# A decode block over 32 heads: one VectorE step moved by a chunk, the last head's exps moved behind copies, and another order of the first head's late sums

## The chip, the core and the metric

The kernel runs on one core of a Trainium2 chip. The metric is the device time of one launch in microseconds (us). TensorE is called PE here, VectorE DVE, ScalarE ACT, GpSimd POOL and SyncE SP, as in the profile.

## The reference

One token `x` (640 numbers) passes an attention block with a cache and then a dense block, in bf16:

```
q = layernorm(x) @ wq                    # 32 heads x 192
p = softmax(q . k_cache * 192**-0.5)     # per head, over 32768 positions
h = x + (p @ v_cache for all heads) @ wo
out = h + relu(layernorm(h) @ w1) @ w2   # 640 -> 1536 -> 640
```

Each head has 12.6 MB of keys and as much of values, so almost all that the kernel does is to read 805 MB of cache, and to make two products with each element.

## The kernel before, in words

**Tiling.** A head has 32768 positions. They are worked in eight *chunks* (`c` = 0 to 7); a chunk holds 32 positions of each of the 128 partitions. Within a chunk two engines share the scores. For 20 or 16 of the 32 positions PE transposes the keys (`transposes`, L366, into `tp`), ACT copies the result out to `kT` (`copies`, L601), and PE multiplies it with the query (`scores_pe`, L397, into `sp`). For the other 12 or 16 positions DVE multiplies keys and query and sums the products (`scores_dve`, L671: the product is L688 and the sum L691, into `sc`). ACT then takes the exp of both parts: `exp_pe` (L610, into `pB`) and `exp_dve` (L616, into `pA`). Last, PE adds exps times values into `o_ps` (`values`, L417): 16 matmuls per chunk, which wait for both exps and for the chunk's values. Where a text says "the sum of chunk c", it means this step; its label in the code is `PV`.

**End of a head.** The output of head h is finished within head h+1: PE adds up the denominators (`den_mm`), DVE scales the output (`den_rec`, L694 and `o_scale`, L699), PE turns the row into a column (`o_turn`, L453), DVE copies the column out (`o_turned`, L707: L709, then L713, which waits for PE's turn, then L715), and PE multiplies it with `wo` (`project`, L460). In PE's order `o_turn` stands behind the scores of chunk 1, and `project` behind the transposes of chunk 4.

**The order of the work** is written out by hand, an order of its own for each engine. Head 0 is built by itself, heads 1 to 30 are one loop (`looped`, L820), head 31 (`LAST`) is built by itself, with ten smaller chunks at its end (`pe_end`, L543). Engines wait for one another on semaphores, and each engine works in its own order, so an instruction that waits holds up all that stand behind it. `SUMS` and `SUMS_0` (L500, L501) say for heads 1 to 30 and for head 0 in which step PE makes which sums. The last entry holds the sums that stand at the very end of a head.

**The transfers** are all issued by SP in one order (`dma_program`, L230): for each head keys `kt[0]` (6 MB, chunks 0 to 3), values `vb` (3 MB, chunks 0 and 1), keys `kt[1]` (6 MB, chunks 4 to 7), then values of chunks 2 and 3 into `vb` again and values of chunks 4 to 7 (6 MB) into `va`. In head 0 alone the load of `va` stands ahead of the second load of `vb`. A load may only be issued when its buffer is free. That is why SP waits for sums: the first load of `vb` for head h waits until the sum of chunk 3 of head h-1 is done (L253), the second until the sum of chunk 1 of the same head is done. The keys `kt[1]` of a head stand behind that first load of `vb` in SP's order. The last head loads smaller pieces, four value pieces behind its sum of chunk 1, and `w1` and `w2` behind its sum of chunk 3.

**Last head.** ACT's order there is that of `act_head` (L644): copies of chunk c, then both exps of chunk c-1. DVE goes through the nine chunks in which it has a part, and PE through `pe_end`. After the last sum come the denominators, the projection, a second layernorm and the dense block: small instructions, one behind the other.

Of the kernel before, what the change touches and what calls it, by code (L numbers as in the profile page):

```python
# [80 lines left out]
def kernel(  # L81
# [34 lines left out]
    LAST = H - 1  # L116
# [13 lines left out]
    def chunks(h):  # L130
        return ends if h == LAST else full
# [285 lines left out]
    def values(g, h, c):  # L417

        jc, jp, ld, off = chunks(h)[c][2:]
        jd = jc - jp  # L420
        if h == LAST and ld >= NL - 1:
            g.wait("vc", h, c)
        elif h == LAST and ld == 2:
            g.wait("vh", c - 4)
        elif off == 0:
            g.wait("at", "v", h, ld)
        g.wait("ep", h, c)
        if jd > 0:
            g.wait("ed", h, c)
        if c == 0 and h > 0:  # L430
            g.wait("os", h - 1)
        src = v_tile(h, ld)
        a, b = pA[c % NB], pB[c % NB]
        calls = []
        order = list(range(jd, jc, 2)) + list(range(0, jd, 2))
        for i, j in enumerate(order):
            w = a[:, j:j + 2] if j < jd else b[:, j - jd:j - jd + 2]
            calls.append(mmul(o_ps[0:2, 0:2 * Dh], w, src[:, (off + j) * Dh:(off + j + 2) * Dh],
                              start=(c == 0 and i == 0),
                              stop=(c == len(chunks(h)) - 1 and i == len(order) - 1), skip_group_check=True))  # L440
        pe_group(g, calls, ("PV", h, c), "pe")

    def den_mm(g, h):
        g.wait("ep", h, len(chunks(h)) - 1)
        if h < LAST:
            g.wait("ed", h, NC - 1)
            g.wait("qm", h + 1)
        else:
            g.wait("ed", h, NCM - 2)
            g.wait("oTc", h - 1)  # L450
        pe_group(g, [mmul(mm[:, 0:2 * NCM], ones_mat[:], dsums[:], start=True, stop=True)], ("den", h), "pe_dve")
# [33 lines left out]
    def q_spread(g, h, turn=None):  # L485

        hh = h if turn is None else turn
        calls = [mmul(mm[:, e:Dh:2], qe[:, bass.ds(2 * hh + e, 1)].to_broadcast([HE, P]), wide[0:HE, HE:2 * HE],
                      start=(e == 0), stop=(e == 1), skip_group_check=True) for e in range(2)]

        for b in range(3):
            for i in range(2):
                j = (P - HE) * b + (HE if i == 0 else 0)
                calls.append(mmul(mm[:, Dh + 4 * b + i:Dh + 4 * b + i + 3:2], wide[0:HE, j:j + P],
                                  qe[:, bass.ds(2 * hh, 2)], start=True, stop=True))
        pe_group(g, calls, ("qs", h), "pe_act")
# [1 line left out]


    SUMS = ((), (), (0,), (1,), (), (), (2, 3), (4,), (5, 6, 7))  # L500
    SUMS_0 = ((), (), (0,), (1,), (), (), (4,), (5,), (6, 7, 2, 3))  # L501

    def pe_head(g, h, turn=None):
        for c in range(NC + 1):
            if c < NC and c != 4:
                transposes(g, h, c)
            if c == 0 and h > 0:
                den_mm(g, h - 1)
            for d in (SUMS if h > 0 else SUMS_0)[c]:
                if c < NC:  # L510
# [9 lines left out]
            if c == 6:  # L520
                q_spread(g, h + 1, turn)
        for d in (SUMS if h > 0 else SUMS_0)[NC]:
            values(g, h, d)
# [77 lines left out]
    def copies(g, h, c):  # L601
        ld, off, jc, jp = chunks(h)[c][:4]
        t0 = sum(len(tiles(q[3])) for q in chunks(h)[:c])
        for k, (b0, nb) in enumerate(tiles(jp)):
            g.wait("T", h, c, k)
            src = tp[(t0 + k) % TP]
            g.do(lambda: act.copy(out=kT[c % 2][:, b0:b0 + nb, :], in_=src[:, 0:nb, :].bitcast(bf16)),  # L607
                 "act_pe", ("cp", h, c, k))

    def exp_pe(g, h, c):  # L610
        jp = chunks(h)[c][3]
        g.wait("S", h, c)
        g.do(lambda: act.activation(out=pB[c % NB][:, 0:jp], in_=sp[:, 0:jp], func=F.Exp, scale=SCALE,  # L613
                                    accum_out=dsums[:, 2 * c + 1:2 * c + 2]), "act_pe", ("ep", h, c))

    def exp_dve(g, h, c):  # L616
        ld, off, jc, jp = chunks(h)[c][:4]
        jd = jc - jp
        if jd == 0:
            return  # L620
        g.wait("sc", h, c)
        g.do(lambda: act.activation(out=pA[c % NB][:, 0:jd], in_=sc[c % NC][:, 0:jd], func=F.Exp, scale=SCALE,  # L622
                                    accum_out=dsums[:, 2 * c:2 * c + 1]), "act_pe", ("ed", h, c))

    def q_wide(g, h):
        g.wait("qs", h)
        if h > 0:
            g.wait("sc", h - 1, NC - 1)
        g.do(lambda: act.copy(out=qb[:], in_=mm[:, 0:Dh]), "act_dve", ("qb", h))
        g.do(lambda: act.copy(out=qm[:], in_=mm[:, Dh:Dh + 12]), "act_pe", ("qm", h))  # L630
# [12 lines left out]

    def act_head(g, h):  # L644
        q_wide(g, h)
        n = len(chunks(h))
        for c in range(n):
            if c == 4 and h < LAST:
                exp_pe(g, h, 3)
                exp_dve(g, h, 3)  # L650
                copies(g, h, 4)
                continue
            copies(g, h, c)
            if c > 0:
                exp_pe(g, h, c - 1)
                exp_dve(g, h, c - 1)
        exp_pe(g, h, n - 1)
        exp_dve(g, h, n - 1)

    def act_end(g):  # L660
        act_head(g, LAST)
        act_norm(g, "ln2")
        g.wait("h1")
        g.wait("rs", "ln2")
        g.do(lambda: act.activation(out=h1T[:], in_=o_ps[:, 0:FT], func=F.Relu, scale=ln_t["ln2"]["rs"][:]),
             "act_pe", ("h1T",))
# [4 lines left out]
    def scores_dve(g, h, c):  # L671
        ld, off, jc, jp = chunks(h)[c][:4]
        jd = jc - jp
        if jd == 0:
            return
        if h == LAST and ld >= NL - 1:
            g.wait("k", h, ld)
        else:
            g.wait("atd", "k", h, ld)
        if c == 0:  # L680
            g.wait("qb", h)
        if h == LAST and c >= NC:
            g.wait("PV", h, c - NC)
        src = k_tile(h, ld)
        n = -(-jd // JDM)
        for i in range(n):
            j0, j1 = jd * i // n, jd * (i + 1) // n
            g.chain(lambda: dve.tensor_tensor(  # L688
                out=pr[:, 0:j1 - j0, :], in0=src[:, (off + j0) * Dh:(off + j1) * Dh].rearrange("p (j d) -> p j d", d=Dh),
                in1=qb[:].unsqueeze(1).to_broadcast([P, j1 - j0, Dh]), op=A.mult), "dve")  # L690
            g.chain(lambda: dve.reduce_sum(out=sc[c % NC][:, j0:j1], in_=pr[:, 0:j1 - j0, :], axis=X), "dve")  # L691
        g.tell("dve_act", ("sc", h, c))

    def den_rec(g, h):  # L694
        g.wait("den", h)
        g.chain(lambda: dve.reduce_sum(out=rec[:, 0:1], in_=mm[:, 0:2 * NCM], axis=X), "dve")  # L696
        g.chain(lambda: dve.reciprocal(out=rec[:, 1:2], in_=rec[:, 0:1]), "dve", ("rec", h))  # L697

    def o_scale(g, h):  # L699
        if h == LAST:  # L700
            g.wait("PV", h, NCM - 1)
        g.wait("rec", h)
        g.do(lambda: dve.tensor_scalar_mul(out=o_pair[:, :, 1, :],  # L703
                                           in0=o_ps[0:2, 0:2 * Dh].rearrange("q (i d) -> q i d", i=2),
                                           scalar1=rec[0:2, 1:2]), "dve_pe", ("os", h))

    def o_turned(g, h):  # L707

        g.chain(lambda: dve.tensor_scalar(out=odd[:], in0=odd[:], scalar1=-1.0, scalar2=1.0, op0=A.mult, op1=A.add),  # L709
                "dve", ("odd", h))  # L710
        g.wait("oT", h)
        g.wait("odd", h)
        g.do(lambda: dve.tensor_scalar_mul(out=oT[:], in0=mm[:, 0:3], scalar1=odd[:]), "dve_pe", ("oTc", h))  # L713
        if h < LAST:
            g.chain(lambda: dve.tensor_copy(out=o_pair[:, :, 0, :], in_=o_pair[:, :, 1, :]), "dve")  # L715
# [27 lines left out]
    def dve_head(g, h):  # L743
        for c in range(len(chunks(h))):
            scores_dve(g, h, c)
            if c % 4 == 3 and h < LAST:
                g.tell("dve_sp", ("scs", h, c))
            if c == 0 and h > 0:
                den_rec(g, h - 1)
                o_scale(g, h - 1)  # L750
            if c == 1 and h > 0:
                o_turned(g, h - 1)

    def dve_end(g):
# [48 lines left out]
    for e in parts:  # L803
        far = {s: 0 for s in TAKEN[e]}
        ends_at[e] = []
        for h in range(LAST):
            for label in logs[e][h]:
                s, n = at[label]
# [86 lines left out]
```

The softmax here doesn't subtract the row's maximum and nothing guards it: scores larger than these inputs give would overflow.

## Time and profile before

| what | us |
|---|---|
| median of 9 runs | 1928.43 |
| lowest and highest run | 1926.48, 1930.83 |
| the profiled execution | 1927.57 |
| span of its instructions | 1925.8 |
| PE, PEld, DVE, ACT busy | 1554.4, 1093.4, 1560.0, 939.5 |

The span runs from the first to the last instruction that the profile has; the profiled execution's own time is 1.8 us longer. PEld is PE's weight loading, which runs beside its matmuls. In rows of the timeline the columns are: start, duration, engine, line, operation, tiles written and read, count, and in brackets the engine's idle time just before and what ended it. Rows of a table by windows give for each stretch its length, the busy time of PE, PEld, DVE, ACT and POOL (with instruction counts), the granted PE clock, the share of time that the sixteen DMA engines were busy, and GB/s.

### The profile page before, as it was taken

The page shows a single profiled execution, that of the slowest core. Times are in us where ns is not written, and L with a number is a line of the kernel's source. Part 1 is how long each engine was busy: PE and PEld are TensorE (multiplying, and loading weights), DVE is VectorE, ACT ScalarE, POOL GpSimd, SP SyncE. Part 2 cuts the span into 40 slices and gives each one's busy share as a digit, 9 for nine tenths or more (in the row PEclk, how much of TensorE's full clock was granted, in tenths as well). Part 3 has the DMA queues.
Part 4 walks back from the last instruction along what each step waited for, and adds up shares of the span by engine and source line. Part 5 has one row for each costly group of instructions (what it writes and reads, how often), then busy time and mean ns, then how long its engine had stood idle before and what let it go on. Part 6 is the DMA issues. An engine that isn't in the chain of part 4 may idle for free.

```text
span 1925.8 us, 36134 instructions
## 1 busy us (share of the span) xinstructions
PE 1554.4 (81%) x15908; PEld 1093.4 (57%) x15908; DVE 1560.0 (81%) x732; ACT 939.5 (49%) x2000; POOL 1.0 (0%) x6
## 2 busy tenths in 40 slices
PE   7878887887888787878788878878777788878797
PEld 7555565665555565555554556555555556555554
DVE  2797787987878978789887879878788787897886
ACT  2454454554544554545544535545445445455453
POOL 0000000000000000000000000000000000000000
PEclk9888988788988879888889888889888898888988
DMA  9999999999999999999999999999999999999997
GB/s 410 419 423 436 426 437 430 436 434 434 431 432 432 437 431 432 438 428 437 436 430 432 438 429 436 436 431 434 434 435 431 435 429 437 429 437 434 434 427 293
DMA packets 29634, 825.29 MB, mean 429 GB/s; under 512 B 3115, under 2 KB 4652, under 8 KB 8108
## 3 DMA queue, kind: packets, MB, share of 16 engines
q1 hardware_dynamic: 29610, 824.98, 99.3%
q8 instruction: 15, 0.25, 0.0%
q14 instruction: 7, 0.06, 0.0%
q10 hardware_dynamic: 2, 0.00, 0.0%
HBM read 824.97 MB, written 0.00 MB: 428 GB/s over the span
## 4 chain that ended last, share of the span: by engine, by line
DVE 41%; DMA 38%; PE 15%; ACT 5%; issue 1%; DVEq 0%; POOLq 0%; SPq 0%
DMA kt<-in_A_k_cache_dram 34%; DVE sc L691 19%; DVE pr L688 19%; PE o_ps L364 7%; PE tp L383 6%; ACT kT L607 4%; DMA va<-in_A_v_cache_dram 2%; DMA vb<-in_A_v_cache_dram 1%; PE sp L364 1%; DVE o_pair L703 1%; ACT pA L622 0%; DVE oT L713 0%; DMA kt<-in_A_wq_dram 0%; DVE rec L696 0%; DVE rec L697 0%
## 5 line engine op out<-in xcount | busy, mean ns | idle before, releaser
L688 DVE TENSOR_TENSOR pr<-kt,qb 128x2304 f32<-128x2304 bf16 (+2 forms) x257 | 755.9, 2941 | 316.7 <-POOLq L325 288.5
L607 ACT COPY kT<-tp 128x1024 bf16<-128x1024 bf16 (+1 forms) x899 | 814.2, 1015 | 270.4 <-PE tp L383 270.3
L383 PE MATMUL tp<-ident_f,kt 128*128 128x128 f32 x3459 | 598.0, 334 | 249.2 <-POOLq L346 173.7
L691 DVE TENSOR_REDUCE sc<-pr 128x12 f32<-128x2304 f32 (+2 forms) x257 | 755.3, 2939 | 8.9
L383 PEld LDWEIGHTS tp<-ident_f,kt 128*128 128x128 f32 x3459 | 492.8, 173 | 304.2 <-POOLq L346 188.1
L364 PE MATMUL o_ps<-va,pB 128*2 128x384 bf16 x1152 | 221.6, 340 | 61.7 <-POOLq L346 61.5
L364 PEld LDWEIGHTS sp<-qm,kT 128*128 128x128 bf16 x6918 | 197.8, 98 | 81.8 <-issue 43.3
L364 PE MATMUL o_ps<-vb,pB 128*2 128x384 bf16 x1154 | 217.0, 335 | 23.3 <-ACT pA L622 20.3
L364 PE MATMUL sp<-qm,kT 128*128 128x2 bf16 x6918 | 214.6, 164 | 25.0 <-ACT pB L613 24.0
L622 ACT ACTIVATE pA<-sc 128x12 bf16<-128x12 f32 (+2 forms) x257 | 57.9, 225 | 354.2 <-DVEq L65 354.2
L613 ACT ACTIVATE pB<-sp 128x20 bf16<-128x20 f32 (+2 forms) x258 | 51.8, 201 | 311.4 <-PE sp L364 311.3
L364 PEld LDWEIGHTS o_ps<-va,pB 128*2 128x2 bf16 x1152 | 94.1, 86 | 157.9 <-POOLq L346 69.3
L364 PE MATMUL o_ps<-va,pA 128*2 128x384 bf16 x896 | 172.6, 334 | 0.0
L364 PE MATMUL o_ps<-vb,pA 128*2 128x384 bf16 x894 | 166.6, 326 | 0.0
L364 PEld LDWEIGHTS o_ps<-vb,pB 128*2 128x2 bf16 x1154 | 91.0, 85 | 125.6 <-ACT pA L622 26.2
L364 PEld LDWEIGHTS o_ps<-va,pA 128*2 128x2 bf16 x896 | 77.4, 86 | 76.2 <-issue 9.8
L364 PEld LDWEIGHTS o_ps<-vb,pA 128*2 128x2 bf16 x894 | 75.2, 84 | 70.6 <-issue 0.6
L613 ACT ACTIVATION_READ_ACCUMULATOR pB<-sp 128x1 f32 x258 | 54.7, 212 | 0.0
L622 ACT ACTIVATION_READ_ACCUMULATOR pA<-sc 128x1 f32 x257 | 52.7, 205 | 0.0
L364 PE MATMUL o_ps<-xn_ln,kt 128*96 128x1 bf16 (+1 forms) x316 | 22.4, 208 | 2.8 <-DMA kt<-in_A_wq_dram 2.8
L364 PEld LDWEIGHTS o_ps<-xn_ln,kt 128*96 128x96 bf16 (+1 forms) x316 | 22.2, 176 | 2.9 <-issue 2.8
L703 DVE TENSOR_SCALAR o_pair<-o_ps,rec 2x384 bf16<-2x384 f32 x32 | 19.3, 605 | 2.7 <-PE o_ps L364 1.7
(69 smaller groups left out, 188.6 us busy)
## 6 DMA issues: line engine op xcount, KB each, us to landing
kt<-in_A_k_cache_dram SPq DMA_DIRECT2D x62, 6144.0 KB, 25.8
vb<-in_A_v_cache_dram SPq DMA_DIRECT2D x63, 3072.0 KB, 24.8
va<-in_A_v_cache_dram SPq DMA_DIRECT2D x31, 6144.0 KB, 26.8
kt<-in_A_k_cache_dram SPq DMA_DIRECT2D x3, 3072.0 KB, 21.0
wo_s<-in_A_wo_dram SPq DMA_DIRECT2D x16, 480.0 KB, 19.0
kt<-in_A_wq_dram SPq DMA_DIRECT2D x4, 1536.0 KB, 11.0
va<-in_A_v_cache_dram SPq DMA_DIRECT2D x1, 3072.0 KB, 25.3
va<-in_A_v_cache_dram SPq DMA_DIRECT2D x2, 1536.0 KB, 36.0
```

The costliest lines, as they stand in the source:

```text
L364: return lambda: pe.matmul(o, lhsT=w, rhs=r, **kw)
L383: calls.append(lambda b=b, o=o: pe.transpose(out=dst[:, b, :], in_=src[:, o:o + 2 * P].bitcast(f32), identity=ident_f[:]))
L607: g.do(lambda: act.copy(out=kT[c % 2][:, b0:b0 + nb, :], in_=src[:, 0:nb, :].bitcast(bf16)), "act_pe", ("cp", h, c, k))
L613: g.do(lambda: act.activation(out=pB[c % NB][:, 0:jp], in_=sp[:, 0:jp], func=F.Exp, scale=SCALE, accum_out=dsums[:, 2 * c + 1:2 * c + 2]), ...
L622: g.do(lambda: act.activation(out=pA[c % NB][:, 0:jd], in_=sc[c % NC][:, 0:jd], func=F.Exp, scale=SCALE, accum_out=dsums[:, 2 * c:2 * c + ...
L688: g.chain(lambda: dve.tensor_tensor(out=pr[:, 0:j1 - j0, :], in0=src[:, (off + j0) * Dh:(off + j1) * Dh].rearrange("p (j d) -> p j d", d=D ...
L691: g.chain(lambda: dve.reduce_sum(out=sc[c % NC][:, j0:j1], in_=pr[:, 0:j1 - j0, :], axis=X), "dve")
L703: g.do(lambda: dve.tensor_scalar_mul(out=o_pair[:, :, 1, :], in0=o_ps[0:2, 0:2 * Dh].rearrange("q (i d) -> q i d", i=2), scalar1=rec[0:2, ...
```

## The change

Three edits, all in the order of the work; no instruction is added or taken away.

1. In head 0 the four sums at its very end go in the order 2, 3, 6, 7 and not 6, 7, 2, 3.
2. In the last head ACT takes the exp of DVE's part of a chunk one step later: after the copies of the chunk after next, and just ahead of the exp of PE's part of the next chunk. In heads 0 to 30 ACT's order stays.
3. In heads 1 to 31 DVE runs `o_turned` behind its scores of chunk 2, and not behind those of chunk 1.

```diff
-    SUMS_0 = ((), (), (0,), (1,), (), (), (4,), (5,), (6, 7, 2, 3))
+    SUMS_0 = ((), (), (0,), (1,), (), (), (4,), (5,), (2, 3, 6, 7))
...
     def act_head(g, h):
...
             copies(g, h, c)
-            if c > 0:
+            if h == LAST:
+                if c > 1:
+                    exp_dve(g, h, c - 2)
+                if c > 0:
+                    exp_pe(g, h, c - 1)
+            elif c > 0:
                 exp_pe(g, h, c - 1)
                 exp_dve(g, h, c - 1)
+        if h == LAST:
+            exp_dve(g, h, n - 2)
         exp_pe(g, h, n - 1)
         exp_dve(g, h, n - 1)
...
             if c == 0 and h > 0:
                 den_rec(g, h - 1)
                 o_scale(g, h - 1)
-            if c == 1 and h > 0:
+            if c == 2 and h > 0:
                 o_turned(g, h - 1)
```

## Prediction

> **What bounds the kernel now.** I read the page's rows by slices first, then tables by windows around every stretch in which the DMA engines are not full, and then the timeline of those stretches.
>
> The page's rows by slices (each slice is 48 us):
>
> ```profile
> DMA  9999999999999999999999999999999999999997
> GB/s 410 419 423 436 426 437 430 436 434 434 431 432 432 437 431 432 438 428 437 436 430 432 438 429 436 436 431 434 434 435 431 435 429 437 429 437 434 434 427 293
> ```
>
> The transfers are the bound from the first slice to the last but one. DVE and PE are 81% busy, but what they lose there they lose waiting for data. Only a stretch in which the DMA engines starve, or the end, can give time. Tables by windows find one hole early on:
>
> ```profile
> 90.00:92.00 2.00, 2.00 (x14) 1.06 (x13) 0.00 (x0) 0.00 (x0) 0.00 (x0) 1.00 1.15 492
> 92.00:94.00 2.00, 2.00 (x14) 1.02 (x13) 0.00 (x0) 0.00 (x0) 0.00 (x0) 1.00 0.91 393
> 94.00:96.00 2.00, 2.00 (x14) 0.92 (x11) 0.00 (x0) 0.00 (x0) 0.00 (x0) 1.00 0.46 197
> 96.00:98.00 2.00, 0.15 (x1) 0.00 (x0) 0.00 (x0) 0.00 (x0) 0.00 (x0) 1.00 0.82 197
> 98.00:100.00 2.00, 1.78 (x9) 1.78 (x10) 1.72 (x1) 0.72 (x1) 0.00 (x0) 0.59 0.75 319
> ...
> 1000.00:1700.00 700.00, 565.68 (x5773) 395.67 (x5774) 580.62 (x264) 349.44 (x740) 0.00 (x0) 0.88 1.00 434
> ```
>
> The last two columns are the DMA share and GB/s. From 94 to 100 us they fall to 197, 197 and 319 GB/s, against 434 in the steady heads. The missing bytes, 2 x (237 + 237 + 115) = 1178 KB, are 2.7 us at 434 GB/s. The timeline there shows why:
>
> ```profile
> 78.67 0.33 SPq L232 DMA_DIRECT2D kt<-in_A_k_cache_dram  x1
> ...
> 85.59 1.79 PE L364 MATMUL o_ps<-va,pB 128*2 128x384 bf16 x10
> ...
> 90.79 1.79 PE L364 MATMUL o_ps<-vb,pB 128*2 128x384 bf16 x10
> ...
> 94.69 1.46 PE L364 MATMUL o_ps<-vb,pA 128*2 128x384 bf16 x8
> 96.18 0.33 SPq L232 DMA_DIRECT2D vb<-in_A_v_cache_dram  x1
> ...
> 98.22 3.37 PE L383 MATMUL tp<-ident_f,kt 128*128 128x128 f32 x15 [2.07 <-POOLq L346]
> ```
>
> SP issues head 1's first values only when head 0's sum of chunk 3, the last of all (reading `vb`), is done at 96.15. The load before it is then all but finished. At the end, the DMA engines fall off after 1910 us, and the last head's engines decide:
>
> ```profile
> 1865.74 0.15 DVE L709 TENSOR_SCALAR odd<-odd 128x1 f32<-128x1 f32 x1
> ...
> 1871.74 0.22 DVE L713 TENSOR_SCALAR oT<-mm,odd 128x3 bf16<-128x3 f32 x1 [5.85 <-PE mm L364]
> ...
> 1896.54 0.21 ACT L622 ACTIVATE pA<-sc 128x16 bf16<-128x16 f32 x1 [4.33 <-DVEq L65]
> ...
> 1897.80 0.69 PE L383 MATMUL tp<-ident_f,kt 128*128 128x128 f32 x2 [4.43 <-ACT kT L607]
> ...
> 1905.85 1.75 DVE L691 TENSOR_REDUCE sc<-pr 128x8 f32<-128x1536 f32 x1
> ...
> 1913.98 0.81 PE L364 MATMUL o_ps<-vb,pB 128*2 128x384 bf16 x4
> ```
>
> DVE stands 5.85 us for PE's turn of the output. Later ACT stands 4.33 us for DVE's scores of chunk 5, and PE 4.43 us for the copies behind that exp. The last sum ends at 1914.8, and 11.0 us of small steps follow.
>
> **Edit 1, the order of head 0's last sums.** Chunks 2 and 3 take the place at 85.59. Their values were issued at 54.64 and landed 26.7 us later (transfers of `vb`), at 81.3, so nothing waits. Two sums take 5.2 us (85.59 to 90.79), so SP issues at 90.98, not 96.18. The single landings of the load before it (issued 78.67) lie from 95.5 to 98.1, median 95.8. The load of 96.18 lands after 10.1 us; its 3.15 MB need 7.25 us at 434 GB/s, so some 2.3 us are start-up (median landing 105.7). Issued at 90.98 it is ready at 93.3, before the first engine runs dry: the hole closes and the median engine gains 2.7 us. Not all of it counts, since a load is done when its latest engine is. The latest one, at 98.1, went on without a gap. Spread behind the median: 2.3 us before the hole, 0.5 behind it, 1.5 from 142 us on, 1.0 at 1850. If the 2.3 stays, the gain is 2.7 - 0.8 = **1.9 us**, which I take as nearest to what the landings show. Bounds: 2.7, if the spread falls back to 1.5; 0.6, if the latest engine falls behind by another 1.3, as others did. Next to be late is the second `vb` load, issued at 114.48 behind DVE's scores: ready at 116.8, while the keys ahead of it now end at 117.2 to 117.6. It fits by 0.4 us. From there to 1700 us I see no hole, so the gain is carried to the last head. Sums 6 and 7 end at 96.15; what waits for them is SP's load of `va`, behind 114.48 anyway.
>
> [...]
>
> **Edit 3 in the loop.** L709 to L715 (1051.38 to 1052.06, 0.7 us) go behind chunk 2, 5.2 us later. In the loop L713 waits for nothing (6.2 us in all, 2 times, both in the last head), so DVE's work is the same. Column `oT` is out at 1057.1, not 1051.9; `project` takes it at 1063.24. Room 6.1 us: nothing. Without that cover PE would wait in every head (rival 4).
>
> **Edits 2 and 3 in the last head.** Times without edit 1. *DVE*: chunk 2 takes the place of the wait, 1865.74 to 1870.9. PE's first sum waits for the exp of DVE's chunk 0, which now stands behind the copies of chunk 2 (3.6 us): 1866.85, not 1866.33. So `o_turn` comes at 1872.1 and L715 ends at 1872.7. Chunk 3 starts there, not at 1877.52: DVE is 4.8 us earlier, and its last scores end at 1902.8 (1907.6 before). *ACT and PE*, with durations of the same rows (a sum 2.7, four copies 3.6, three 2.8, an exp with its read 0.35):
>
> | step | before | after | what it waits for |
> |---|---|---|---|
> | sum 1 | 1873.1 | 1876.05 | exp of DVE's chunk 1, now behind copies 3 |
> | transposes 4 | 1876.5 | 1879.5 | sum 1, scores 2 |
> | sum 2 | 1881.35 | 1884.0 | copies 4, then its exp |
> | sum 3 | 1887.0 | 1888.8 | PE's own order |
> | copies 7 | 1896.75 | 1892.75 | transposes 7, no longer DVE's chunk 5 |
> | sum 4 | 1901.1 | 1896.8 | PE's own order |
> | scores 9 | 1906.0 | 1900.5 | PE's own order |
> | sums 5, 6, 7, 8, 9 | 1906.4 to 1914.8 | 1900.9 to 1909.2 | PE alone: 2.6, 1.6, 1.6, 0.4 for the denominators, 2.0 |
>
> Up to sum 3 the edits *lose* 2 to 3 us. They win it back where ACT no longer stands for DVE. From 1889 on PE is never idle for long, so PE sets the end, **5.6 us** earlier. The last DVE exp, at 1903.1, is needed at 1906.8. Data: `w2` lands by 1912.9 (issued 1895.84, 17.1 us), and the last products would start at 1914.1. The loads of `w1` and `w2` are issued 1.7 us later (behind sum 3), while the queue holds values until 1903.3: nothing. Value pieces are issued 3 us later behind sum 1, while loads are queued until 1895: nothing.
>
> **PE's clock** is the open price. Between transposes 3 and sum 1 PE now idles 2.45 us. After an idle of 2.07 (98.22) fifteen transposes took 3.37 us with the granted clock at 0.59; after one of 1.89 (1096.25) they took 1.86 at 1.00. So sum 1 may run slow: at most 1.6 us. I take half, **0.8 us**. The other way, sum 0 may escape the half clock (3.26 us for ten matmuls now, 1.79 elsewhere): 1.5 us more gain.
>
> [...]
>
> **Sum** against the profiled execution: 1927.57 - 1.9 - 5.6 + 0.8 = 1920.9. The median of the runs is 0.86 above that execution, so I forecast 1921.7. Best case 2.7 + 5.6 + 1.5 = 9.8, or 1918.6; worst case 0.6 + 4.0 = 4.6, or 1923.8.
>
> **Rivals.**
> 1. *The hole closes for nothing*: the latest DMA engine has no gap, so if it sets every landing and falls behind further, only the tail gains: 4.8 us, 1923.6. For it: the latest landing at 98.1. Against it: the spread of 0.5 behind the hole.
> 2. *PE becomes the tail's bound at half clock*: the sums held behind copies leave PE idle at 1873.6 and around 1882. A half clock of 6.8 us, as from 1897 to 1904 before (0.50), costs 3.4 us: 1927.57 - 1.9 - 5.6 + 3.4, or 1924.3 by the median, and 1926.2 if rival 1 holds too. Against it: the gaps are shorter than the 4.43 us that went before that stretch.
> 3. *L713 waits all the same*: `o_turn` hangs on the values that land at 1866.2. It does, by 0.8 us; that is in the sum.
> 4. *Slower*: the late column holds PE in the loop. `project` stands ahead of the transposes and the sums that release the next keys. Those are issued at 1074.61, and the loads ahead of them end at about 1080.5, less 2.3 of start-up: 3.6 us of room. From 6.1 + 3.6 = 9.7 us of delay on, each further us costs 30 heads x 1 us: about 1951 for one. The rows show 5.2, so it is unlikely.
>
> **How the numbers follow.** Forecast 0.69, rival 1 0.12, rival 2 0.15, rival 4 0.04. A measurement can tell some 0.2% (3.9 us) from no change. Beyond it lie nine tenths of the forecast (0.63), three quarters of rival 1 (0.09) and two thirds of rival 2 (0.10): faster 0.82, within 0.14, slower 0.04. The range goes from the best case to rival 2's first figure, with 0.4 and 0.7 us for the runs' scatter: 1918.2 to 1925.0.
>
> **What would show it.** Head 1's first `vb` load issued near 91.0, and no slice under 390 GB/s from 94 to 100; loads 1.9 us earlier at 1000 us. In the last head L709 behind chunk 2's sum, no wait of ACT for DVE over 1 us at chunk 5, and the last sum 5 us earlier relative to the head's first keys. Wrong would be: landings at 1850 unmoved, or PE's sums at 0.33 us per matmul after 1880.

## The result, and the profile after

The changed kernel takes 1921.49 us (median of 9 runs, 1920.34 to 1923.47) against 1928.51 us of the kernel before in the same comparison. The ratio is 0.9965, with a 95% interval from 0.9956 to 0.9973. The forecast was 1921.7. Its profiled execution took 1921.55 us, with a span of 1919.7 us, 6.1 us less than before's. (Edits move the later line numbers by 8: L709, L713 and L691 of before are L717, L721 and L699 here.)

The page's row of GB/s by slices of the changed kernel:

```profile
GB/s 409 427 433 429 428 437 430 438 433 432 433 433 431 435 434 429 437 429 437 434 433 433 432 434 435 433 429 437 430 437 434 433 430 435 430 435 436 427 434 335
```

The second and third slices (48 to 144 us) now show 427 and 433 GB/s, where before they showed 419 and 423; the last shows 335, not 293. Those are the two places where the prediction looked. The table by windows of the changed kernel (the last two columns are the DMA share and GB/s):

```profile
94.00:96.00 2.00, 2.00 (x14) 1.03 (x13) 0.00 (x0) 0.00 (x0) 0.00 (x0) 1.00 1.11 479
96.00:98.00 2.00, 0.86 (x6) 0.25 (x3) 0.00 (x0) 0.00 (x0) 0.00 (x0) 1.00 0.89 381
98.00:100.00 2.00, 1.65 (x15) 1.65 (x16) 1.59 (x1) 0.96 (x2) 0.00 (x0) 1.00 1.00 430
...
116.00:118.00 2.00, 0.54 (x22) 0.45 (x19) 1.70 (x5) 0.47 (x4) 0.00 (x0) 0.67 0.78 307
118.00:120.00 2.00, 0.00 (x0) 0.00 (x0) 2.00 (x1) 0.00 (x0) 0.00 (x0) 0.50 0.87 352
```

The hole from 94 to 100 is closed (430 GB/s over the three windows). A smaller one has opened from 116 to 120, where before there were 442 and 418 GB/s: against 434 GB/s (127 + 82) x 2 = 418 KB are missing, 1.0 us. It is the place where the prediction left 0.4 us of room. The timeline of the changed kernel around the first hole:

```profile
86.30 1.79 PE L364 MATMUL o_ps<-vb,pB 128*2 128x384 bf16 x10
...
91.50 1.79 PE L364 MATMUL o_ps<-va,pB 128*2 128x384 bf16 x10
91.69 0.33 SPq L232 DMA_DIRECT2D vb<-in_A_v_cache_dram  x1
```

Chunks 2 and 3 (`vb`) are summed first without a wait, and SP issues 4.5 us earlier than before. The timeline of the last head, one row of before and then the changed kernel:

```profile
1851.84 2.56 DVE L688 TENSOR_TENSOR pr<-kt,qb 128x2304 f32<-128x2304 bf16 x1 [1.70 <-POOLq L325]
```

```profile
1851.18 2.56 DVE L696 TENSOR_TENSOR pr<-kt,qb 128x2304 f32<-128x2304 bf16 x1 [1.67 <-POOLq L325]
...
1865.10 2.56 DVE L696 TENSOR_TENSOR pr<-kt,qb 128x2304 f32<-128x2304 bf16 x1
...
1872.32 0.22 DVE L721 TENSOR_SCALAR oT<-mm,odd 128x3 bf16<-128x3 f32 x1 [1.77 <-PE mm L364]
...
1876.00 1.46 PE L364 MATMUL o_ps<-vb,pB 128*2 128x384 bf16 x8 [2.26 <-ACT pA L622]
...
1894.64 0.24 ACT L622 ACTIVATE pA<-sc 128x16 bf16<-128x16 f32 x1
...
1901.06 1.75 DVE L699 TENSOR_REDUCE sc<-pr 128x8 f32<-128x1536 f32 x1
...
1907.90 0.81 PE L364 MATMUL o_ps<-vb,pB 128*2 128x384 bf16 x4
```

DVE starts chunk 2 straight after chunk 1. Its wait for the turned column falls from 5.85 to 1.77 us. The exp of DVE's chunk 5 (1894.64) no longer shows a wait; it was 4.33 us. Sum 1 (1876.00) stands 2.26 us for its exp (2.45 in the prediction). From the first DVE scores of the last head (1851.84 before, 1851.18 now) to the end of the span it is 73.95 us before and 68.49 now. So of the 6.1 us the last head gave 5.5, and all that lies ahead of it 0.66.

### The profile page after: what moved, and what is told of

Read it like the earlier page. It is cut to its first block, busy times and chain, and to the rows that moved or that the text cites. A ratio compares the mean times of both kernels' runs of the same rounds, so it can differ in the third digit from the quotient of the medians.

```text
span 1919.7 us, 36134 instructions
## 1 busy us (share of the span) xinstructions
PE 1548.2 (81%) x15908; PEld 1086.7 (57%) x15908; DVE 1560.0 (81%) x732; ACT 939.4 (49%) x2000; POOL 1.0 (0%) x6
## 4 chain that ended last, share of the span: by engine, by line
DVE 39%; DMA 38%; PE 16%; ACT 5%; issue 1%; DVEq 0%; POOLq 0%; SPq 0%
DMA kt<-in_A_k_cache_dram 34%; DVE sc L699 19%; DVE pr L696 18%; PE o_ps L364 8%; PE tp L383 7%; ACT kT L607 5%; DMA va<-in_A_v_cache_dram 2%; DMA vb<-in_A_v_cache_dram 1%; PE sp L364 1%; DVE o_pair L711 1%; ACT pA L622 1%; DVE oT L721 0%; DMA kt<-in_A_wq_dram 0%; DVE rec L704 0%; DVE rec L705 0%
## 5 line engine op out<-in xcount | busy, mean ns | idle before, releaser
L699 DVE TENSOR_REDUCE sc<-pr 128x12 f32<-128x2304 f32 (+2 forms) x257 | 755.3, 2939 | 8.9
L383 PEld LDWEIGHTS tp<-ident_f,kt 128*128 128x128 f32 x3459 | 487.1, 172 | 301.7 <-POOLq L346 187.5
L364 PE MATMUL o_ps<-xn_ln,kt 128*96 128x1 bf16 (+1 forms) x316 | 22.3, 208 | 2.8 <-DMA kt<-in_A_wq_dram 2.7
## 6 DMA issues: line engine op xcount, KB each, us to landing
vb<-in_A_v_cache_dram SPq DMA_DIRECT2D x63, 3072.0 KB, 24.8
va<-in_A_v_cache_dram SPq DMA_DIRECT2D x1, 3072.0 KB, 24.8
```

The costliest lines, as they stand in the source:

```text
L364: return lambda: pe.matmul(o, lhsT=w, rhs=r, **kw)
L383: calls.append(lambda b=b, o=o: pe.transpose(out=dst[:, b, :], in_=src[:, o:o + 2 * P].bitcast(f32), identity=ident_f[:]))
```

## The experiments

Two questions were open: what edit 1 is worth, since this one trace shows 0.66 and not 1.9 us; and which of edits 2 and 3 wins the last head. "First DVE scores" below are those of the last head; times after them are counted from there, so that what came before drops out.

**Each edit alone.** The first is the diff of the `SUMS_0` line and nothing else:

```diff
-    SUMS_0 = ((), (), (0,), (1,), (), (), (4,), (5,), (6, 7, 2, 3))
+    SUMS_0 = ((), (), (0,), (1,), (), (), (4,), (5,), (2, 3, 6, 7))
```

> Only edit 1 (head 0's last sums in the order 2, 3, 6, 7). The prediction's term: 1.9 us faster than before, with head 1's first vb load issued near 91.7 us as in the changed kernel, no slice under 390 GB/s from 94 to 100 us, and the last head's first DVE scores near 1850 (1851.84 before). Rival, taken from the changed kernel's trace: the hole moves on to 116 to 120 us, where the second vb load comes late, and the latest DMA engine keeps its lag; then 0.6 us, and the last head's first DVE scores near 1851.2.

1926.13 us against 1928.42, ratio 0.9989 (0.9980 to 0.9998). Its table by windows, and the first DVE scores in its timeline:

```profile
94.00:96.00 2.00, 2.00 (x15) 1.03 (x13) 0.00 (x0) 0.00 (x0) 0.00 (x0) 1.00 0.80 344
96.00:98.00 2.00, 0.89 (x6) 0.34 (x5) 0.05 (x1) 0.00 (x0) 0.00 (x0) 1.00 0.91 393
98.00:100.00 2.00, 2.00 (x20) 2.00 (x21) 2.00 (x1) 1.41 (x2) 0.00 (x0) 1.00 0.97 418
116.00:118.00 2.00, 0.08 (x4) 0.00 (x0) 1.85 (x2) 0.47 (x4) 0.00 (x0) 0.68 0.87 365
118.00:120.00 2.00, 0.05 (x1) 0.05 (x1) 2.00 (x1) 0.00 (x0) 0.00 (x0) 0.50 0.90 381
```

```profile
1850.07 2.56 DVE L688 TENSOR_TENSOR pr<-kt,qb 128x2304 f32<-128x2304 bf16 x1 [1.68 <-POOLq L325]
```

The first hole is mostly gone (344 GB/s is left in one window), the second is there as well ((69 + 53) x 2 = 244 KB, 0.6 us), and the last head starts 1.77 us earlier than before. So the recorded 1.9 us came nearly in full in this execution, in spite of the second hole.

The second is the new order in `act_head` alone:

```diff
             copies(g, h, c)
-            if c > 0:
+            if h == LAST:
+                if c > 1:
+                    exp_dve(g, h, c - 2)
+                if c > 0:
+                    exp_pe(g, h, c - 1)
+            elif c > 0:
                 exp_pe(g, h, c - 1)
                 exp_dve(g, h, c - 1)
+        if h == LAST:
+            exp_dve(g, h, n - 2)
```

> Only edit 2 (in the last head the exps of DVE's scores behind the next copies); DVE still stands for the turned output after chunk 1. If edit 2 is what wins the tail, because ACT no longer stands for DVE (the prediction's reading of its table), about 4 us faster. If DVE sets the tail, its last scores still end at 1907.6 and sums 5 to 8 follow the exps of DVE's chunks 5 to 8 one by one: copies 9 wait behind the exp of chunk 6 and scores 9 behind that of chunk 7 (1904), so the last sum ends near 1913, 1.8 us faster, and ACT's idle time before L622 in the last head stays above 10 us.

1929.25 us against 1928.42, ratio 1.0004 (0.9995 to 1.0013): nothing, and not even the 1.8 us of the second reading. (In its one profile the time from the first DVE scores to the end is 72.6 us against 73.95, 1.3 us less, which the medians do not show.) Its waits in the last head are nearly what that reading expected: ACT and DVE still stand, ACT for 9.7 us and not over 10 (the columns are total, times, longest):

```profile
ACT pA L622 <- DVEq L65: 9.7, 5, 3.3
DVE oT L721 <- PE mm L364: 6.2, 1, 6.2
```

The third is the one line in `dve_head`:

```diff
-            if c == 1 and h > 0:
+            if c == 2 and h > 0:
                 o_turned(g, h - 1)
```

> Only edit 3 (DVE copies the turned output out behind chunk 2); ACT's order in the last head as before. If edit 2 is needed to use DVE's head start, at most 2 us faster. If DVE's late start was all of it, 5.5 us faster: DVE's chunk 5 ends near 1891 and not 1896.4, so ACT's wait of 4.33 us and PE's of 4.43 us shrink below 1 us by themselves, sum 1 stays at 1873 and the last sum ends near 1909.3. In the loop nothing changes: project still at 23 to 25 us after the head's first keys, landings of the keys at 1000 us unmoved.

1923.94 us against 1928.42, ratio 0.9974 (0.9963 to 0.9984): 4.5 us in the medians, 5.0 by the ratio. Edits 2 and 3 together give no more (next run), so this is the tail's gain as far as run times can tell. Its timeline of the last head:

```profile
1871.27 0.22 DVE L713 TENSOR_SCALAR oT<-mm,odd 128x3 bf16<-128x3 f32 x1 [0.21 <-PE mm L364]
...
1872.62 1.46 PE L364 MATMUL o_ps<-vb,pB 128*2 128x384 bf16 x8
...
1890.71 0.22 ACT L622 ACTIVATE pA<-sc 128x16 bf16<-128x16 f32 x1
...
1898.09 0.21 ACT L622 ACTIVATE pA<-sc 128x8 bf16<-128x8 f32 x1 [1.83 <-DVEq L65]
...
1900.01 0.48 PE L364 MATMUL sp<-qm,kT 128*128 128x2 bf16 x12 [2.28 <-ACT pB L613]
...
1909.27 0.81 PE L364 MATMUL o_ps<-vb,pB 128*2 128x384 bf16 x4
```

The wait of ACT at chunk 5 (1890.71) is gone with ACT's old order: DVE is simply done earlier. Sum 1 keeps its old place (1872.62). What is left to edit 2 is the 2.28 us of scores 9, which stand behind the copies that stand behind the exp of DVE's chunk 7 (1898.09).

**Edits 2 and 3 without edit 1** (the two diffs above together):

> Edits 2 and 3 without edit 1. The prediction's terms: 4.8 us faster (5.6 if sum 1 runs at the full clock). With the hole of head 0 still there (head 1's first vb load at 96.2), the last head's first DVE scores stay at 1851.8; if they move earlier too, part of what I put down to edit 1 is not its own.

1923.71 us against 1928.42, ratio 0.9974 (0.9964 to 0.9984), the same as edit 3 alone. The first DVE scores stand at 1852.6, so in this execution they do not come earlier without edit 1.

**Edits 1 and 3 without edit 2:**

> Edits 1 and 3 without edit 2. If edit 2 does nothing beside edit 3, the time of the changed kernel, 1921.5. If it is worth the 0.9 us that the traces of edit 3 alone and of the whole change show in the last head (last sum 57.6 and 56.7 us after the head's first DVE scores), 1922.4. If the prediction's reading held that edit 2 is what wins the tail, over 1924.

1921.28 us against 1929.34, ratio 0.9954 (0.9940 to 0.9967): the changed kernel's time. Beside edit 3, edit 2 adds nothing that run times can tell. The traces leave room for 1 us: from the first DVE scores to the end it is 69.3 and 69.6 us in the two kernels with edit 3 and without edit 2, and 68.5, 68.5, 68.5, 69.0 and 70.2 in the five kernels whose last head has both. But in each of the two without edit 2 a sum ran in part at half clock (2.72 us for eight matmuls in one, 3.36 for ten in the other; 1.46 and 1.79 elsewhere), so the difference need not be edit 2's. In this profile (1923.30 us, the slowest of its five runs) the first DVE scores stand at 1851.94, no earlier than before, although edit 1 is in.

**Late exps only from chunk 4 on**, to keep edit 2's win without its loss:

```diff
             if h == LAST:
-                if c > 1:
+                if c > 5:
                     exp_dve(g, h, c - 2)
                 if c > 0:
                     exp_pe(g, h, c - 1)
+                if 0 < c < 5:
+                    exp_dve(g, h, c - 1)
```

> The whole change, but in the last head the exps of DVE's chunks 0 to 3 stand where they stood before, and only those from chunk 4 on come behind the next copies. If edit 2 loses at sums 0 to 3 (sum 1 3 us late behind copies 3) and wins at scores 9 (2.3 us of waiting behind the exp of chunk 7), this keeps the win without the loss: sum 1 at 21 and not 24.8 us after the head's first DVE scores, the last sum near 53.6 and not 56.7, and 2.5 us less than the changed kernel, about 1919, where the landing of w2 becomes the next bound. If the early loss is hidden (DVE or the value loads set sums 4 to 9), the time stays at 1921.5.

1920.73 us against 1929.34, ratio 0.9954 (0.9941 to 0.9968). By the ratios this is no different from the change; the 1919 that I expected did not come. Sum 1 is back at 21.3 us after the first DVE scores; the last sum starts at 55.2 (56.7 in the changed kernel), not at the 53.6 that I expected. Scores 9 still stood 1.53 us behind the exp of chunk 7.

**The old place in the loop**, the new one in the last head alone (`if c == (2 if h == LAST else 1) and h > 0:`):

> The whole change, but in heads 1 to 30 DVE copies the turned output out behind chunk 1 as before; behind chunk 2 only in the last head. The prediction's claim that the move costs and gains nothing in the loop: 1921.5, within 0.1%. If the loop's move is worth something, at least 0.1 us per head, or 3 us.

1921.32 us against 1929.34, ratio 0.9956 (0.9943 to 0.9970): the loop's move is worth nothing, as the prediction had it. So all of edit 3's gain is one wait in one head of 32.

**The column still later in the loop**, behind chunk 3 and behind chunk 4 (`2 if h == LAST else 3`, and `else 4`):

> The whole change, but in heads 1 to 30 DVE copies the turned output out behind chunk 3 (last head: behind chunk 2). Second dose for rival 4: the column comes near 26.3 us after the head's first DVE scores, and project's turn is at 25.0, but the transposes behind it wait for ACT's copies until 27.2 anyway: no change, within 0.1% of the changed kernel. If each late column costs time, as behind chunk 4 (0.75 us per head), at least 0.3 us x 30 = 9 us.

> The whole change, but in heads 1 to 30 DVE copies the turned output out behind chunk 4, some 18 us later than before (last head: behind chunk 2). Dose for the prediction's rival 4. By its rule (9.7 us of room, 30 us for each further one) 8.6 x 30, near 2180. By the timeline of the loop: the column comes near 31.9 us after the head's first DVE scores and not 13.6, project waits for it, and the transposes behind it start 5 us later (not 8.6, since they wait for ACT's copies as it is); of these 3.6 are room, so each head loses 1.4 us: some 42 us, near 1963. If the loads have more room than I think, no change.

Behind chunk 3: 1921.68 us against 1928.84, ratio 0.9965 (0.9952 to 0.9978). There the column is out 25.9 us after the head's first DVE scores, where before it was 13.6, so 12.3 us of delay are free. Behind chunk 4: 1943.82 us against 1929.34, ratio 1.0060 (1.0043 to 1.0077); its three runs lie from 1936.33 to 1944.43. The waits of the whole execution and the timeline of head 17 in the kernel with chunk 4:

```profile
PE attT L364 <- DVE oT L721: 181.6, 31, 6.3
```

```profile
1080.41 0.56 PE L364 MATMUL attT<-oT,wo_s 128*128 128x1 bf16 x15 [6.03 <-DVE oT L721]
...
1089.18 0.33 SPq L232 DMA_DIRECT2D kt<-in_A_k_cache_dram  x1
```

PE stands some 6 us in every head for the column, which is out at 31.2 us, 17.6 us later than before. The next head's keys are then issued 40.0 us after the head's first DVE scores (1049.18), where before it was 36.3; on average over heads 2 to 27 it is 40.2 against 36.7. The mechanism of rival 4 is real, but its price is 22.3 us over the changed kernel in the medians, or 0.75 us per head (14.8 us in the fastest of the three runs). Keys 3.5 to 3.7 us late cost 0.75, so an estimate of the loads' room is some 3 us, and not 3.6.

**The change again, and the last exps swapped**, on one chip. The second moves, on top of the kernel with late exps from chunk 4, the exp of PE's chunk ahead of DVE's in the two last steps:

```diff
-                if c > 5:
+                if 5 < c < 8:
                     exp_dve(g, h, c - 2)
                 if c > 0:
                     exp_pe(g, h, c - 1)
+                if c > 7:
+                    exp_dve(g, h, c - 2)
```

> The whole change again, unaltered, on the chip of the two runs beside it: 1921.5 if the chip is like the first one. If the first DVE scores of the last head stand anywhere between 1850.0 and 1851.9 and follow the lag of the latest DMA engine at the last head's first keys (1.0 us: early, 2.0 us or more: late), then what edit 1 is worth differs from execution to execution; if they stand at 1851.2 with another lag, the lag is not the reason.

> The kernel with late exps from chunk 4 on, and in the two last steps the exp of PE's chunk ahead of the late exp of DVE's: scores 9 then no longer wait behind the exp of DVE's chunk 7 (1.5 us there). If PE sets the end from sum 4 on, the last sum starts near 53.7 us after the head's first DVE scores and not 55.2, and the time falls by another 1.4 us, about 2.5 below the changed kernel. If w2's landing (near 1911 to 1912) ends the gain, products with w2 wait for it and less than 0.5 us is won.

The change again: 1920.66 us (1920.24 to 1921.94) against 1928.84, ratio 0.9958 (0.9945 to 0.9972); first DVE scores at 1850.03. The swapped one: 1919.30 us (1917.69 to 1921.76), ratio 0.9952 (0.9938 to 0.9965). Its timeline:

```profile
1896.23 0.45 PE L364 MATMUL sp<-qm,kT 128*128 128x2 bf16 x12 [0.36 <-ACT pB L613]
...
1896.85 0.21 ACT L622 ACTIVATE pA<-sc 128x8 bf16<-128x8 f32 x1 [0.67 <-DVEq L65]
...
1904.18 0.81 PE L364 MATMUL o_ps<-vb,pB 128*2 128x384 bf16 x4
```

Scores 9 now wait 0.36 us. The last sum starts at 54.1 us after the first DVE scores, 2.7 us earlier than in the change. In the medians it is 1.4 us, the lowest of all kernels here, but the ranges overlap, so that it beats the change is likely and not proved.

## Why the prediction was right

**The size** was right, 6.7 us from three terms against 7.0 in the medians and 6.1 between the spans of the two profiled executions. The terms did not all do so well.

**Edit 1** (1.9 us, bounds 0.6 and 2.7): alone it was 2.3 us in the medians, with an interval of 0.4 to 3.9; 1.77 in its own profile, 0.66 in that of the change. Part of that difference lies ahead of the edit. SP issues head 1's first keys (at 78.67 before) before anything that the three edits touch, and yet that issue stands anywhere from 78.2 to 79.4 in the twelve profiles (all but the kernel with chunk 4, whose loop is slower). Counted from it, the four kernels with the hole agree within 0.2 us. In the table the *lag* is how far the latest of the sixteen landings of the last head's first keys is behind their median:

| kernel | issue | first DVE scores of the last head | between | lag |
|---|---|---|---|---|
| before | 78.67 | 1851.84 | 1773.17 | 1.04 |
| edit 2 | 79.08 | 1852.35 | 1773.27 | 1.03 |
| edit 3 | 78.36 | 1851.71 | 1773.35 | 1.05 |
| edits 2 and 3 | 79.35 | 1852.61 | 1773.26 | 1.10 |
| the change | 79.38 | 1851.18 | 1771.80 | 1.69 |
| the change again | 78.76 | 1850.03 | 1771.27 | 1.24 |
| edit 1 | 79.31 | 1850.07 | 1770.76 | 0.97 |
| edits 1 and 3 | 79.26 | 1851.94 | 1772.68 | 1.51 |
| late exps from chunk 4 | 78.55 | 1851.03 | 1772.48 | 1.95 |
| last exps swapped | 78.21 | 1850.13 | 1771.92 | 1.55 |
| old place in the loop | 79.32 | 1850.04 | 1770.72 | 0.87 |
| behind chunk 3 | 78.98 | 1850.33 | 1771.35 | 1.53 |

So edit 1 brought 0.6 to 2.5 us, 1.6 on average, and 1.5 in the changed kernel, whose load happened to be issued 0.7 us late. In each of the twelve the first DVE scores start 0.15 us behind the latest landing. The gain falls as the lag grows: 2.5 us with lags of 0.9 and 1.0, 2.0 with 1.2, 1.3 to 1.9 with 1.5 to 1.7, 0.8 with 2.0. That is the prediction's mechanism and its bounds. One kernel does not fit, edits 1 and 3 with 0.6 us at a lag of 1.5: its latest landing was 3.2 us behind at 155 us, and from 176 to 178 us the transfers fell to 258 GB/s; whether the one made the other stays open. Rival 1, *the hole closes for nothing*, came near in that one execution of eight: its last head started no earlier than before's.

The hole itself was sized rightly: from the median landing of the load ahead of it to that of head 1's first `vb` load it was 9.92 us before and 7.27 in the change, 2.65 us less, where the prediction had 2.7. Two other steps of this term were off. The second `vb` load did not fit with 0.4 us to spare: in the changed kernel it lands 7.66 us behind the keys ahead of it, 7.27 before, by the medians of the landings, so 0.4 us were lost there (in the kernel with edit 1 alone it is 7.30, nearly nothing). And the lag of 2.3 us did not stay: at the last head it is 0.9 to 2.0. Up to 160 us it rises in single steps of as much as 1.6 us; from there to the last head it rose by over 0.25 us at once only twice in the twelve profiles. Ten of the 15 packets of 16 KB on the instruction queue fall into the first 160 us (in before and in the change); that these packets make the steps was not tried.

**Edit 3 in the loop** (nothing): right, by the run with the old place in the loop and by the one with chunk 3.

**Edits 2 and 3 in the last head** (5.6 us at full clock): right in size and nearly in each step. In the changed kernel sums 1, 2, 3, 4 and 5 start at 24.8, 32.8, 37.4, 45.3 and 49.1 us after the first DVE scores. The prediction's table, from its 1851.84, says 24.2, 32.2, 37.0, 45.0 and 49.1. From first DVE scores to the end it is 5.5 us less. Rival 3's wait was 1.77 us and not 0.8, so that DVE was 4.1 us earlier and not 4.8; PE's sums came nearly as in the table all the same.

**Where it was wrong**: the sentence "They win it back where ACT no longer stands for DVE" and the table's "no longer DVE's chunk 5" credit ACT's new order with what DVE's head start does. I worked out edits 2 and 3 as one and never asked what edit 3 does with the old order. Edit 3 alone won 4.5 us in the medians; edit 2 alone won nothing, and nothing beside edit 3 that the medians show. It holds sums 0 to 3 behind copies (sum 1 by 2.3 us of idle PE), and gives that back once, at scores 9. Of the signs that the prediction named, one failed: loads 1.9 us earlier at 1000 us (head 17's first DVE scores stand at 1037.60, 0.67 us earlier), and one just failed: no window under 390 GB/s from 94 to 100 (381 in one).

**PE's clock** (0.8 us, half of 1.6): it was either, not half. In the changed kernel and in the kernel with edit 2 alone PE idles the same 2.26 us before sum 1. The tables by windows, the change first (the clock is third from the end):

```profile
1873.70:1876.00 2.30, 0.04 (x2) 0.00 (x1) 2.30 (x1) 2.25 (x5) 0.00 (x0) 1.00 0.94 406
1876.00:1879.40 3.40, 3.40 (x44) 1.97 (x45) 3.37 (x2) 0.00 (x0) 0.00 (x0) 1.00 0.97 415
```

```profile
1873.90:1876.20 2.30, 0.14 (x2) 0.00 (x0) 2.27 (x2) 2.30 (x5) 0.00 (x0) 1.00 1.04 449
1876.20:1877.40 1.20, 1.10 (x7) 0.59 (x8) 1.20 (x1) 0.05 (x1) 0.00 (x0) 1.00 0.95 410
1877.40:1880.80 3.40, 3.40 (x23) 1.35 (x21) 3.25 (x2) 0.00 (x0) 0.00 (x0) 0.50 0.95 408
```

In the one, 44 matmuls follow in 3.4 us at full clock; in the other 23 at half clock, and sum 1 takes 4.3 us and not 2.7. The traces show a pattern. Every stretch of full or of half clock between two changes lasts a whole multiple of 3.41 us (at half clock 3.41, 6.83, 10.24 or 13.65 us in the changed kernel), so in these traces the clock changes at steps of that length. In the kernel with edit 2 alone the whole idle (1874.04 to 1876.30) lies within one step, 1873.99 to 1877.40, in which PE was 34% busy; the next step ran at half clock. In the change a step ends inside the idle, at 1874.56, so that it is shared by two steps that were 76% and 58% busy, and the clock stayed full. Six profiles have this idle of 2.26 us: in two it lies within one step, and half clock followed; in four it is shared, and the clock stayed full. Where the steps fall differs from execution to execution, so the surcharge is one of chance. In the change it fell away, and edit 1's small 0.66 in that execution made up for it: two errors of the sum that nearly cancel (1.2 us too much for the gain, of which head 0's late start was 0.7, and 0.8 too much for the clock).

**Rival 4** was priced wrongly: 30 us per us beyond 9.7 us of delay would have made 77 us of chunk 3 (12.3 us of delay), where nothing came, and 236 us of chunk 4 (17.6), where 22.3 came. Its step "project stands ahead of the transposes" holds, but those transposes wait for ACT's copies as well (1.62 us in head 17 before), so only 3.5 to 3.7 us of the delay reached the keys.

## What to carry to other kernels

When a change has several parts, work the path out for each part alone: a wait that ends because its producer is earlier looks just like one that ends because its consumer was moved. In a kernel that the transfers bound, look for the few stretches with fewer GB/s, and ask for each what the next load waits for; after closing one hole, compute the room of the next load too: here the earlier transfers used it up, and from 116 to 120 us 307 and 352 GB/s were left of 442 and 418. A step that is free in a loop need not stay free when it comes later still: here 12.3 us of delay cost nothing and 17.6 us cost 0.75 us per head, and that price followed the 3.5 to 3.7 us that reached the next load's issue, not the delay itself.

## What the runs showed of the hardware

PE's clock, as granted, was 1.00 or 0.50 and changed only at steps of 3.41 us. The same PE idle of 2.26 us was followed by half clock where it lay within one step (two executions, the step 34% busy) and by full clock where two steps shared it (four executions; in the changed kernel they were 76% and 58% busy). The busy share of a step alone does not tell which: in before and the changed kernel steps 45% busy kept the full clock, and some 80% busy were followed by half.

A load of the cache has sixteen landings (head 1's first keys before: from 95.57 to 98.13 us, median 95.83), and in the last head of twelve profiles the first DVE scores started 0.15 us behind the latest of them. From 300 us to the last head the latest landing was 1.7 to 1.9 us behind the median in the changed kernel; before, that distance went from 1.5 to 1.0 us. The bytes that were missing in the starved stretch, worth 2.7 us at 434 GB/s, were not its price: closing it brought 0.6 to 2.5 us.
